# Undivided float32 operands for the first two token blocks of an attention and two-layer feed-forward kernel

## Chip, cores and metric

One core of a Trainium2 chip. The time is the device time of one execution in microseconds; 1083.91 us is the median of three runs of the kernel before (1081.91 to 1086.0).

## The reference, cut to what matters

Causal attention with a forget-gate decay for 4 batches, 8 heads, 576 positions and head size 64; its output, 2304 tokens by 512, goes through two feed-forward layers with 2048 inner columns each.

```python
scores = scale * q @ k.T + cum[:, None] - cum[None, :]     # causal, cum = cumsum(log f)
x = (softmax(scores) @ v)                                  # 2304 x 512
h = x @ w_in;   g = h * clip(h + 3, 0, 6) / 6;   x = g @ w_out
h = x @ w2_in;  g = where(h >= 1, h, where(h <= -1, 0, (h + 1) ** 2 / 4));  out = g @ w2_out
```

All of it is float32.

## The kernel before, in words

**Precision.** Most products are made on a reduced float32 type (`fp32r` in the profile), which TensorE takes in one pass. To keep the precision, both operands are divided into a rounded half and a remainder, `hi = round(a)` on ScalarE (`rounded`, line 121) and `lo = a - hi` on VectorE (`rest`, line 129), and a product is three matmuls: hi.hi, lo.hi, hi.lo (lines 560 and 607). A few products in attention (`dc` line 282, `sc` of the first jobs line 378, `av` line 474) take plain float32.

**Layers.** Layer 1 goes over 9 blocks of 256 tokens and 16 chunks of 128 inner columns: a step is one chunk of one block. `moe_h` makes `hp` (4 products of 128x128 by 256 columns), then u on ScalarE (line 567) and VectorE (line 568), then the halves of `g`. `moe_o` adds 4 products of g and the second weight to the block's sums two steps later (`LAG = 2`). After chunk 16 the sums go through `osb` (lines 627 and 625) to `x2d` in DRAM. Layer 2 takes blocks of 512 tokens in the same manner.

**Order.** `steps` holds (block, place, chunk). Blocks 0 and 1 are interleaved: block 1 follows block 0 by nine chunks (`STAG`), so that the first 32 steps, numbers 0 to 31, take both; blocks 2 to 8 follow one after another, the chunks forwards and backwards in turn. Attention is cut into pieces (scores, transposes, output) that are put between the half steps by a list of costs and due times (`cost`, `due`, `goal`); the pieces for block 0 come first of all. A scheduler places each engine's instructions from that order.

**Weights.** They come as 64-bit numbers: `w_load("raw")` fetches half a chunk (512 KB, line 157, at most four buffers `wraw`) and `w_split` converts it in a tile `wr` (ScalarE line 178, VectorE lines 179, 183, 186 and 189). For layer 1 the halves are then made into one of 12 slots `w` of 2 x 8 x 128 columns; `plan_weights` decides which chunk a slot holds at which step. Chunks that must be loaded again are kept as halves in DRAM (`wf`, `w_keep`, line 200, 1 MB) and come back by line 160. For layer 2 the converted `wr` goes to DRAM undivided through POOL's queue (line 194), in chunks from step 38 to step 105, and is loaded and divided in layer 2 ("whole"). `wr` has two buffers, which `osb` shares.

**Queues.** SP issues the loads and most stores in order. POOL makes the masks of attention (`affine_select`, lines 302, 306 and 315), which wait for the `dec` loads, and issues line 194's stores between them.

Of the kernel before, what the change touches and what calls it, by code (L numbers as in the profile page):

```python
# [8 lines left out]
F32 = mybir.dt.float32  # L9
# [7 lines left out]
P = 128  # L17
NCH = DFF // P
KD = DM // P
# [28 lines left out]
def plan_weights(visits, avail):  # L48
# [9 lines left out]
    chunk, nuse, used = [None] * n, [10**9] * n, [a - LAG - 1 if a else -LAG - 1 for a in avail]  # L58
    for t, c in enumerate(visits):
# [15 lines left out]
def tile_kernel(  # L75
# [39 lines left out]
    wsb = [wpool.tile([P, 2, 8, P], F32R, name=f"w{s}") for s in range(SLOTS)]  # L115
# [17 lines left out]
    for i in range(NCH + STAG):  # L133
        if i < NCH:
            steps.append((0, i, i))
        if i >= STAG:
            steps.append((1, i - STAG, i - STAG))
    for j in range(2, NB2):
# [4 lines left out]
    where, loads = plan_weights([c for _, _, c in steps], [0] * SLOTS + [g7] * MORE)  # L143
# [7 lines left out]
    for c, _, _, _ in loads:  # L151
        again[c] = again.get(c, -1) + 1

    def w_load(kind, c, half, s):
        if kind == "raw":
            raw = att.tile([P, 4 * P, 2], I32, tag="wraw", name="wraw", bufs=WRAW)
            nc.sync.dma_start(out=raw, in_=w[c // NCH, c % NCH, :, 8 * P * half:8 * P * half + 8 * P])
            return raw
        if kind == "parts":
            nc.sync.dma_start(out=wsb[s].bitcast(F32), in_=wf[c])  # L160
        else:
            nc.sync.dma_start(out=wsb[s][:, 1].bitcast(F32), in_=wf[c])

    def w_split(kind, c, half, s, raw):
        if kind == "parts":
            return
        if kind == "whole":
# [25 lines left out]
        if s is None:  # L193
# [269 lines left out]
    def u_out(p):  # L463
# [16 lines left out]
        for j in range(t0 // T, (t1 - 1) // T + 1):  # L480
            if (j, g) not in xt:
                xt[j, g] = moe1.tile([P, 2, T], F32R, tag="xt", name="xt", bufs=XT)
# [68 lines left out]
    def moe_h(g):  # L551
# [3 lines left out]
        ws = wsb[where[g]]  # L555
        hp = bank("hp")
        hp = hp[:, 0:w]
        for k in range(KD):
            x = xt[j, k]
            for a, bb in ((0, 0), (1, 0), (0, 1)):  # L560
                nc.tensor.matmul(  # L561
                    hp, lhsT=ws[:, a, k], rhs=x[:, bb, 0:w], start=(k == 0 and a == 0 and bb == 0),
                    stop=(k == KD - 1 and bb == 1),
                )
        u = ffn.tile([P, T2[0] if layer else T], F32, tag="u", name="u", bufs=2)[:, 0:w]
        if layer == 0:
            nc.scalar.activation(out=u, in_=hp, func=AF.Relu, bias=3.0, scale=1.0)  # L567
            nc.vector.scalar_tensor_tensor(out=u, in0=u, scalar=6.0, in1=hp, op0=ALU.min, op1=ALU.mult)  # L568
# [18 lines left out]
    def moe_o(g):  # L587
# [3 lines left out]
        ws = wsb[where[g]]  # L591
# [5 lines left out]
        if layer == 0:  # L597
# [82 lines left out]
    wq, seen = [], set()  # L680
    for c, s, free, need in loads:
# [3 lines left out]
        elif c in seen:  # L685
            wq.append((free, free, "parts", c, None, s))
        else:
            seen.add(c)
            t = free if free > 0 else max(-1, need - 6)
            wq += [(t - 3, t, "raw", c, half, s) for half in range(2)]  # L690
# [84 lines left out]
    for g in range(len(steps) + LAG):  # L775
# [74 lines left out]
```

## Time and profile before

| | |
|---|---|
| median of 3 runs | 1083.91 us |
| profiled execution, its own time | 1085.11 us |
| its span, first to last instruction | 1083.4 us |
| mean granted TensorE clock | 0.974 |
| busy: TensorE / VectorE / ScalarE / POOL | 1034.3 / 591.8 / 541.5 / 89.8 us |

In the profile PE is TensorE, DVE is VectorE, ACT is ScalarE, POOL is GpSimd, SP is the engine whose queue issues DMAs; L561 is line 561. PEclk is the granted share of TensorE's full clock, 1.00 for 2.4 GHz and 0.50 for 1.2 GHz. A busy time of TensorE is modelled at the ends of matmuls: back-to-back matmuls are best read from the starts of successive groups. Layer 1 with attention ends and layer 2 begins at about 682 us.

### The profile page before, as it was taken

The numbers are of one execution on the slowest core, as the hardware profiler recorded it, in microseconds if no ns is written. First come the engines' busy times: TensorE is split into PE (matmuls) and PEld (weight loads), VectorE is DVE, ScalarE is ACT, GpSimd is POOL, SyncE is SP. The second block draws the span as 40 slices with busy tenths as digits, with TensorE's granted clock in tenths as the row PEclk, the third lists the DMA queues.
The fourth block names the chain that finished last, engine by engine and source line by source line (L and its number), as shares of the span: only waits on it lengthen the run. The fifth ranks groups of instructions, "written<-read, shape, count | busy, mean of one in ns | idle before, by whom it ended". The sixth has DMA issues, their size and how long they took to land.

```text
span 1083.4 us, 18101 instructions
## 1 busy us (share of the span) xinstructions
PE 1034.3 (95%) x6556; PEld 903.9 (83%) x6556; DVE 591.8 (55%) x1510; ACT 541.5 (50%) x1330; POOL 89.8 (8%) x223
## 2 busy tenths in 40 slices
PE   7987999989799989999999999999999999999998
PEld 5776989979688889888989999888888888888887
DVE  7999984766577776777653436422422322332232
ACT  6877755656456655556553235533333333333343
POOL 2200010111021111121101000000100100000000
PEclk8688999999999999999999999999999999999999
DMA  8976681783586686864826035200200200010010
GB/s 235 337 222 185 213 299 54 226 277 111 182 282 197 202 298 185 282 212 123 249 68 253 2 96 167 90 1 1 77 1 1 72 6 1 19 39 1 1 40 20
DMA packets 69785, 144.20 MB, mean 133 GB/s; under 512 B 11584, under 2 KB 38720, under 8 KB 65600
## 3 DMA queue, kind: packets, MB, share of 16 engines
q1 hardware_dynamic: 67136, 134.66, 39.6%
q0 software_dynamic: 2560, 8.39, 2.0%
q8 instruction: 51, 0.84, 0.3%
q14 instruction: 38, 0.31, 0.1%
HBM read 116.74 MB, written 26.29 MB: 132 GB/s over the span
## 4 chain that ended last, share of the span: by engine, by line
PE 69%; DMA 15%; DVE 7%; issue 4%; ACT 4%; SPq 1%; POOL 0%; DVEq 0%; ACTq 0%; POOLq 0%
PE hp L561 31%; PE o L608 12%; PE o L615 10%; PE ps L615 8%; DMA qraw<-in_q 5%; DMA dec<-ncum 3%; PE pt L432 3%; DMA kraw<-in_k 2%; PE av L474 2%; DMA wraw<-in_w 2%; PE sc L388 1%; DMA x2d<-osb 1%; DMA wf<-wr 1%; DVE prob L339 1%; DVE wr L186 1%
## 5 line engine op out<-in xcount | busy, mean ns | idle before, releaser
L608 PE MATMUL o<-g,w 128*128 128x256 f32 x1728 | 250.3, 289 | 16.8 <-ACT g L121 15.3
L561 PE MATMUL hp<-xt,w 128*128 128x256 f32 x1728 | 250.6, 292 | 7.8 <-ACT w L121 5.1
L608 PEld LDWEIGHTS o<-g,w 128*128 128x128 f32 x1728 | 225.9, 191 | 26.7 <-ACT g L121 19.2
L561 PEld LDWEIGHTS hp<-xt,w 128*128 128x128 f32 x1728 | 226.8, 194 | 14.5 <-ACT w L121 6.1
L561 PE MATMUL hp<-x,w 128*128 128x512 f32 (+1 forms) x960 | 211.4, 369 | 0.0
L561 PEld LDWEIGHTS hp<-x,w 128*128 128x128 f32 x960 | 169.1, 188 | 32.5
L572 DVE SCALAR_TENSOR_TENSOR u<-hp,u 128x512 f32<-128x512 f32 (+1 forms) x80 | 50.8, 637 | 195.9 <-ACT u L571 195.9
L129 DVE TENSOR_TENSOR g<-u,g 128x256 fp32r<-128x256 f32 (+1 forms) x224 | 112.8, 505 | 71.5 <-ACT g L121 71.1
L121 ACT ACTIVATE g<-u 128x256 fp32r<-128x256 f32 (+1 forms) x224 | 106.1, 475 | 88.4 <-DVE u L572 55.3
L570 ACT ACTIVATE u<-hp 128x512 f32<-128x512 f32 (+1 forms) x80 | 44.6, 557 | 173.3 <-PE hp L561 171.5
L615 PE MATMUL o<-w,g 128*128 128x512 f32 x480 | 125.0, 396 | 0.0
L615 PEld LDWEIGHTS o<-w,g 128*128 128x128 f32 x480 | 89.1, 188 | 19.9
L345 ACT ACTIVATE prob<-prob,mx 128x512 f32<-128x512 f32 (+4 forms) x144 | 83.5, 581 | 37.4 <-DVE mx L339 37.0
L615 PE MATMUL ps<-w,g 128*128 128x512 f32 x384 | 100.4, 396 | 0.0
L568 DVE SCALAR_TENSOR_TENSOR u<-u,hp 128x256 f32<-128x256 f32 x144 | 59.4, 416 | 53.8 <-ACT u L567 53.2
L567 ACT ACTIVATE u<-hp 128x256 f32<-128x256 f32 x144 | 53.8, 378 | 67.2 <-PE hp L561 65.4
L615 PEld LDWEIGHTS ps<-w,g 128*128 128x128 f32 x384 | 72.3, 188 | 17.4
L432 PE MATMUL pt<-ident,prob 128*128 128x128 f32 (+1 forms) x400 | 69.1, 296 | 12.6 <-DVE prob L417 12.1
L339 DVE CUSTOM_DVE_ANT_0 prob<-sc,dec 128x256 f32<-128x256 f32 (+1 forms) x112 | 58.8, 533 | 25.1 <-PE sc L388 11.9
L121 ACT ACTIVATE pt<-pt 128x512 f32<-128x512 f32 (+3 forms) x160 | 61.9, 433 | 18.7 <-PE pt L432 18.2
L432 PEld LDWEIGHTS pt<-ident,prob 128*128 128x128 f32 (+1 forms) x400 | 50.3, 150 | 18.4 <-DVE prob L417 12.8
L178 ACT ACTIVATE wr<-wraw 128x512 f32<-128x512 f32 x64 | 43.0, 671 | 44.5 <-DMA wf<-wr 19.0
(76 smaller groups left out, 975.5 us busy)
## 6 DMA issues: line engine op xcount, KB each, us to landing
wraw<-in_w SPq DMA_DIRECT2D x64, 512.0 KB, 6.4
w<-wf SPq DMA_DIRECT2D x24, 1024.0 KB, 8.5
dec<-ncum SPq DMA_DIRECT2D x45, 256.0 KB, 6.6
kraw<-in_k SPq DMA_DIRECT2D x64, 144.0 KB, 3.8
wf<-w SPq DMA_DIRECT2D x8, 1024.0 KB
wf<-wr POOLq DMA_DIRECT2D x32, 256.0 KB, 6.0
w<-wf SPq DMA_DIRECT2D x16, 512.0 KB, 4.1
vv<-in_v SPq DMA_DIRECT2D x16, 320.0 KB, 10.6
```

What stands on the lines that cost most here:

```text
L121: nc.scalar.activation(out=out, in_=in_, func=AF.Copy)
L129: e.tensor_tensor(out=out, in0=in_, in1=hi.bitcast(F32), op=ALU.subtract)
L339: nc.vector.tensor_tensor_reduce(out=py[:, a:e], in0=s, in1=dc, scale=-0.125, scalar=mx[:, 2 * z:2 * z + 1] if x else 3.0e38, op0=ALU.add, ...
L345: nc.scalar.activation(out=py, in_=py, func=AF.Exp, scale=-1.0, bias=mx[:, 2 * z + x:2 * z + x + 1], accum_out=sm[:, z:z + 1],)
L432: nc.tensor.transpose(t[:nk, o:o + P], p[:, c:c + nk], ident)
L561: nc.tensor.matmul(hp, lhsT=ws[:, a, k], rhs=x[:, bb, 0:w], start=(k == 0 and a == 0 and bb == 0), stop=(k == KD - 1 and bb == 1),)
L567: nc.scalar.activation(out=u, in_=hp, func=AF.Relu, bias=3.0, scale=1.0)
L568: nc.vector.scalar_tensor_tensor(out=u, in0=u, scalar=6.0, in1=hp, op0=ALU.min, op1=ALU.mult)
L570: nc.scalar.activation(out=u, in_=hp, func=AF.Relu, bias=0.5, scale=0.5)
L572: nc.vector.scalar_tensor_tensor(out=u, in0=hp, scalar=1.0, in1=u, op0=ALU.max, op1=ALU.min)
L608: nc.tensor.matmul(o, lhsT=ws[:, a, KD + k], rhs=gg[:, bb], start=False, stop=(n == NCH - 1 and bb == 1 and k % 2 == 1),)
L615: nc.tensor.matmul(acc[j][k], lhsT=gg[:, bb, k * P:(k + 1) * P], rhs=ws[:, a, KD:2 * KD].rearrange("p k n -> p (k n)"), start=(n == 0 and ...
```

## The change

- In blocks 0 and 1 the products take undivided float32 operands, one matmul each: the weights from `nat` (8 tiles, each of two whole chunks, in the place of the slots 0 to 7), x and g without a remainder.
- `w_split` converts a layer-1 chunk straight into `nat`. After a chunk's step in block 1, `w_halves` makes its two halves (1024 columns at a time) into a slot, for the blocks from 2 on. Eleven chunks find a slot so (0 to 6, 8, 10, 12, 14); 7, 9, 11, 13 and 15 are kept undivided in DRAM (`w_keep`, 512 KB) and are loaded and divided once at need ("first"), written back as halves if they are needed again (four of them are, and so are chunks 0 to 3 after `w_halves`).
- The chunk order of blocks 2 to 8 follows from that (`back`), and `plan_weights` starts from the slots as block 1 leaves them: 41 loads in the plan instead of 56, of which 20 instead of 24 are halves of layer 1 of 1 MB.
- The raw loads and conversions of layer 1 come six steps before the chunk's step in block 0 for every chunk (chunks 12 to 15 came when a slot was free, at steps 13, 15, 17 and 19; now at 9, 11, 13 and 15).
- `wr` and `osb` share three buffers instead of two.

The diff, cut:

```diff
+    nat = [wpool.tile([P, 2, 8, P], F32, tag=f"w{s}", name=f"wn{s}") for s in range(NCH // 2)]
+    wsb = [None] * SLOTS
...
+    for c in range(NCH):
+        if spare:
+            split[c] = spare.pop(0)
+        else:
+            dropped.append(c)
+        if c % 2:
+            spare.append(c // 2)
...
+    back = [*split, *dropped]
     for j in range(2, NB2):
-        order = range(NCH) if j % 2 else range(NCH - 1, -1, -1)
+        order = back[::-1] if j % 2 else back
...
+        elif kind == "first":
+            nc.sync.dma_start(out=wsb[s][:, 1].bitcast(F32), in_=wf[c][:, 1])
...
+            if kind == "first" and again[c] > 1:
+                nc.sync.dma_start(out=wf[c], in_=wsb[s].bitcast(F32))
...
-        r = moe.tile([P, 4, P], F32, tag="wr", name="wr", bufs=2)
+        if c < NCH:
+            r = nat[c // 2][:, c % 2, ks]
+        else:
+            r = moe.tile([P, 4, P], F32, tag="wr", name="wr", bufs=3)
...
-        else:
-            rounded("a", wsb[s][:, 0, ks], r)
-            rest("v", wsb[s][:, 1, ks], r, wsb[s][:, 0, ks])
-
-    def w_keep(c, s):
-        nc.sync.dma_start(out=wf[c], in_=wsb[s].bitcast(F32))
+
+    def w_keep(c):
+        nc.sync.dma_start(out=wf[c][:, 1], in_=nat[c // 2][:, c % 2])
+
+    def w_halves(c):
+        s = split[c]
+        wsb[s] = wpool.tile([P, 2, 8, P], F32R, tag=f"w{s}", name=f"w{s}")
+        r = nat[c // 2][:, c % 2]
+        rounded("a", wsb[s][:, 0], r)
+        rest("v", wsb[s][:, 1], r, wsb[s][:, 0])
+        if c in again:
+            nc.sync.dma_start(out=wf[c], in_=wsb[s].bitcast(F32))
...
+            if j < 2:
+                rounded("a", x[:, 0, a - j * T:e - j * T], t[:, a - t0:e - t0])
+                continue
...
+            if j < 2:
+                nc.tensor.matmul(hp, lhsT=ws[:, k], rhs=x[:, 0], start=k == 0, stop=k == KD - 1)
+                continue
...
+            if j < 2:
+                gg = ffn.tile([P, 2, T], F32, tag="g", name="g", bufs=3)
+                nc.vector.scalar_tensor_tensor(out=gg[:, 0], in0=u, scalar=6.0, in1=hp, op0=ALU.min, op1=ALU.mult)
+                gt[g] = gg
+                return
...
+                if j < 2:
+                    nc.tensor.matmul(
+                        o, lhsT=ws[:, KD + k], rhs=gg[:, 0], start=False, stop=n == NCH - 1 and k % 2 == 1,
+                    )
+                    continue
...
-                o = moe.tile([P, 512], F32, tag="wr", name="osb", bufs=2)
+                o = moe.tile([P, 512], F32, tag="wr", name="osb", bufs=3)
...
+    for g, (j, _, c) in enumerate(steps[:g2]):
+        if j == 0:
+            t = max(-1, g - 6)
+            wq += [(t - 3, t, "raw", c, half, None) for half in range(2)]
...
-                    if j == 0 and again[c]:
-                        w_keep(c, where[g - LAG])
+                    if j == 0 and c in dropped:
+                        w_keep(c)
+                    if j == 1 and c in split:
+                        w_halves(c)
```

## Rows read from the trace of the kernel before

**Rows 1.** The page: busy us, share of the span, instructions; VectorE's tenths in 40 slices.
```profile
PE 1034.3 (95%) x6556; PEld 903.9 (83%) x6556; DVE 591.8 (55%) x1510; ACT 541.5 (50%) x1330; POOL 89.8 (8%) x223
...
DVE  7999984766577776777653436422422322332232
```
**Rows 2.** Windows: stretch, length, busy us of PE, PEld, DVE, ACT, POOL, clock, DMA share, GB/s.
```profile
0.00:45.00 45.00, 36.74 (x154) 25.25 (x154) 37.17 (x126) 33.29 (x99) 8.76 (x25) 0.73 0.89 277
45.00:150.00 105.00, 90.01 (x650) 81.19 (x649) 100.16 (x264) 76.37 (x201) 9.62 (x20) 0.93 0.73 225
150.00:193.00 43.00, 42.66 (x336) 39.74 (x335) 23.68 (x68) 22.34 (x62) 4.03 (x13) 1.00 0.42 144
193.00:330.00 137.00, 125.86 (x949) 112.61 (x949) 91.53 (x267) 77.20 (x215) 19.75 (x53) 0.98 0.70 218
330.00:585.00 255.00, 245.16 (x1886) 223.37 (x1885) 173.06 (x515) 148.01 (x426) 35.08 (x94) 0.98 0.64 204
```
**Rows 3.** Groups by shape (busy us, mean ns): 45 to 150 us; 0 to 45; whole span.
```profile
L129 DVE TENSOR_TENSOR w<-wr,w 128x512 fp32r<-128x512 f32 x24 | 16.4, 684 | 0.3 <-ACT w L121 0.3
L129 DVE TENSOR_TENSOR g<-u,g 128x256 fp32r<-128x256 f32 x21 | 8.8, 427 | 0.2
...
L129 DVE TENSOR_TENSOR xt<-av,xt 128x256 fp32r<-128x256 f32 x7 | 2.9, 412 | 0.7 <-ACT xt L121 0.7
...
L129 DVE TENSOR_TENSOR w<-wr,w 128x512 fp32r<-128x512 f32 x7 | 4.8, 684 | 0.2 <-ACT w L121 0.2
...
L129 DVE TENSOR_TENSOR w<-w 128x1024 fp32r<-128x1024 f32 x16 | 19.6, 1226 | 20.6 <-ACT w L121 20.6
...
L121 ACT ACTIVATE w<-w 128x1024 fp32r<-128x1024 f32 x16 | 17.0, 1061 | 20.9 <-DMA w<-wf 20.9
```
**Rows 4.** Timeline of TensorE in the steady stretch: start us, us, group.
```profile
608.43 1.60 PE L561 MATMUL hp<-xt,w 128*128 128x256 f32 x12
609.87 1.60 PE L608 MATMUL o<-g,w 128*128 128x256 f32 x12
```
**Rows 5.** Timeline of TensorE at the `dc` matmuls; the window around them.
```profile
11.50 1.57 PE L282 MATMUL dc<-upper,lf 128*128 128x256 f32 x8 [1.62 <-DVE mx L339]
13.01 0.49 PE L378 MATMUL sc<-kn,qn 64*128 64x128 f32 x4
...
12.26 0.38 PE L282 MATMUL dc<-upper,lf 128*128 128x256 f32 x1
...
12.69 0.27 PE L282 MATMUL dc<-upper,lf 128*128 128x128 f32 x1
...
12.20:12.80 0.60, 0.60 (x5) 0.55 (x5) 0.60 (x4) 0.60 (x4) 0.00 (x0) 1.00 0.60 140
```
**Rows 6.** Waits of TensorE, 45 to 193 us: us in total, times, longest.
```profile
PE o L608 <- ACT g L121: 8.7, 6, 2.3
PE hp L561 <- ACT w L121: 5.1, 3, 3.5
```
**Rows 7.** What line 178 waited for; TensorE's stops; a window after one.
```profile
  DMA wf<-wr: 19.0, 7
  DMA x2d<-osb: 12.1, 6
...
224.15 1.74 PE L608 MATMUL o<-g,w 128*128 128x256 f32 x10 [2.78 <-ACT g L121]
...
296.82 0.44 PE L432 MATMUL pt<-ident,prob 128*128 128x128 f32 x2 [3.57 <-DVE prob L417]
...
457.54 0.54 PE L432 MATMUL pt<-ident,prob 128*128 128x128 f32 x2 [2.70 <-DVE prob L417]
...
225.60:229.00 3.40, 3.40 (x15) 3.16 (x15) 2.73 (x10) 2.14 (x6) 1.36 (x3) 0.50 0.64 156
```
**Rows 8.** DMA issues of the first 45 us: KB each.
```profile
wf<-w SPq DMA_DIRECT2D x3, 1024.0 KB
```

More of the change, by code (lines that the diff above doesn't have):

```diff
@@ L45, with plan_weights @@
 AHEAD = 8100
-def plan_weights(visits, avail):
+def plan_weights(visits, avail, start):
     nxt, last = [None] * len(visits), {}
@@ L58, in plan_weights @@
     chunk, nuse, used = [None] * n, [10**9] * n, [a - LAG - 1 if a else -LAG - 1 for a in avail]
+    for s, (c, t) in start.items():
+        chunk[s], used[s] = c, t
+        if c is not None:
+            held[c], nuse[s] = s, last.get(c, 10**9)
     for t, c in enumerate(visits):
@@ L114, in tile_kernel @@
     ncum = dram.tile([B * H, S], F32, name="ncum")
-    wsb = [wpool.tile([P, 2, 8, P], F32R, name=f"w{s}") for s in range(SLOTS)]
+    nat = [wpool.tile([P, 2, 8, P], F32, tag=f"w{s}", name=f"wn{s}") for s in range(NCH // 2)]
+    wsb = [None] * SLOTS
     ident = const.tile([P, P], F32, name="ident")
@@ L137, in tile_kernel @@
             steps.append((1, i - STAG, i - STAG))
+    g2 = len(steps)
+    seen1 = {c: g for g, (j, _, c) in enumerate(steps) if j == 1}
+    split, dropped, spare = {}, [], list(range(NCH // 2, SLOTS))
+    for c in range(NCH):
[5 more added lines that the diff above has]
+            spare.append(c // 2)
+    start = {s: (c, seen1[c] - g2) for c, s in split.items()}
+    start.update({s: (None, seen1[NCH - 1] - g2) for s in spare})
+    back = [*split, *dropped]
     for j in range(2, NB2):
-        order = range(NCH) if j % 2 else range(NCH - 1, -1, -1)
+        order = back[::-1] if j % 2 else back
         for n, c in enumerate(order):
@@ L142, in tile_kernel @@
     g7 = (NB - 2) * NCH
-    where, loads = plan_weights([c for _, _, c in steps], [0] * SLOTS + [g7] * MORE)
+    where, loads = plan_weights([c for _, _, c in steps[g2:]], [0] * SLOTS + [g7 - g2] * MORE, start)
+    where = [None] * g2 + where
+    loads = [(c, s, free + g2, need + g2) for c, s, free, need in loads]
     again = {}
     for c, _, _, _ in loads:
-        again[c] = again.get(c, -1) + 1
+        again[c] = again.get(c, 0) + 1
     def w_load(kind, c, half, s):
@@ L158, in w_load @@
             return raw
+        if s is not None and kind != "raw" and wsb[s] is None:
+            wsb[s] = wpool.tile([P, 2, 8, P], F32R, tag=f"w{s}", name=f"w{s}")
         if kind == "parts":
             nc.sync.dma_start(out=wsb[s].bitcast(F32), in_=wf[c])
+        elif kind == "first":
+            nc.sync.dma_start(out=wsb[s][:, 1].bitcast(F32), in_=wf[c][:, 1])
         else:
@@ L166, in w_split @@
             return
-        if kind == "whole":
+        if kind != "raw":
             lo = wsb[s][:, 1]
@@ L192, in w_split @@
         )
-        if s is None:
+        if c >= NCH:
             nc.gpsimd.dma_start(out=wf[c][:, ks], in_=r)
-        else:
-            rounded("a", wsb[s][:, 0, ks], r)
-            rest("v", wsb[s][:, 1, ks], r, wsb[s][:, 0, ks])
-    def w_keep(c, s):
-        nc.sync.dma_start(out=wf[c], in_=wsb[s].bitcast(F32))
+    def w_keep(c):
+        nc.sync.dma_start(out=wf[c][:, 1], in_=nat[c // 2][:, c % 2])
+    def w_halves(c):
+        s = split[c]
+        wsb[s] = wpool.tile([P, 2, 8, P], F32R, tag=f"w{s}", name=f"w{s}")
+        r = nat[c // 2][:, c % 2]
[3 more added lines that the diff above has]
+            nc.sync.dma_start(out=wf[c], in_=wsb[s].bitcast(F32))
     jobs, pairs = [], []
@@ L481, in u_out @@
             if (j, g) not in xt:
[L482 removed]
+                xt[j, g] = moe1.tile([P, 2, T], F32R if j > 1 else F32, tag="xt", name="xt", bufs=XT)
             x = xt[j, g]
             a, e = max(t0, j * T), min(t1, j * T + T)
+            if j < 2:
+                rounded("a", x[:, 0, a - j * T:e - j * T], t[:, a - t0:e - t0])
+                continue
             rounded("a", x[:, 0, a - j * T:e - j * T], t[:, a - t0:e - t0])
@@ L554, in moe_h @@
         w = T2[j - NB] if layer else T
-        ws = wsb[where[g]]
+        ws = nat[c // 2][:, c % 2] if j < 2 else wsb[where[g]]
         hp = bank("hp")
@@ L590, in moe_o @@
         t0 = sum(T2[:j - NB]) if layer else j * T
-        ws = wsb[where[g]]
+        ws = nat[c // 2][:, c % 2] if j < 2 else wsb[where[g]]
         gg = gt.pop(g)
@@ L684, in tile_kernel @@
             wq.append((free, min(free + 4, need - 2), "whole", c, None, s))
-        elif c in seen:
+        elif c in dropped and c not in seen:
+            seen.add(c)
+            wq.append((free, min(free + 4, need - 2), "first", c, None, s))
+        else:
             wq.append((free, free, "parts", c, None, s))
[L687 to L690, printed above, removed]
     first = list(dict.fromkeys(c for c, _, _, _ in loads if c >= NCH))
```

## The prediction

> **What bounds the kernel now.** I read the page first, then the windows by stage, then the instructions of each stage. The page [rows 1] says TensorE 95% busy and VectorE 55%, which looks like a TensorE kernel; but the VectorE slices (27 us each) show two regimes: 9 tenths or more in slices 2 to 5, 4 in slice 7. The windows [rows 2] make that exact. From 45 to 150 us VectorE is busy 100.2 of 105 us, while TensorE has gaps and a mean granted clock of 0.93. From 150 to 193 us it turns round: TensorE 42.7 of 43, VectorE 23.7. From 193 to 585 us TensorE is busy 92 to 96% and the rest are stalls. Before 45 us VectorE (37.2 of 45), ScalarE and the DMA engines (0.89) are all close to full. The 32 steps that the change touches (blocks 0 and 1) run from about 45 to 193 us: 21 remainders of g, one for each step, lie in the first window [rows 3], the other 11 in the second.
>
> So the change trades VectorE work, which is the limit up to 150 us, for TensorE work, which is the limit from 150 us on. Its third buffer acts after 193 us.
>
> **TensorE, the price.** A divided product is three matmuls of 256 columns. In the steady stretch twelve of them start at 608.43 and the next twelve at 609.87 [rows 4]: 1.44 us, 0.120 us each, 0.36 us for three. The undivided product is a plain float32 matmul, which the trace records as two per call. Its nearest row is the `dc` matmul, the same 128x128 by 256 columns: a call starts at 12.26 and the next at 12.69, at a granted clock of 1.00 (2.4 GHz) [rows 5]. That is 0.43 us a call, 0.07 more than three divided ones. With 8 calls in a step (4 for hp, 4 for o) a step costs 8 x 0.43 - 24 x 0.12 = 0.59 us more, 32 steps 18.9 us more. Bounds: from below the same 0.43, since the two starts stand in one unbroken stream; from above the whole group with its start, 1.51 us from 11.50 to 13.01 for 768 columns [rows 5], 0.50 us per 256, which would make the 32 steps 18 us dearer still. Four calls follow each other in a step, so I take the stream.
>
> One page disagrees with the row. The Trainium skill, Perfetto Trace Analysis, section Engine Utilization, gives float32 low/high half the output rate of the array; by that an undivided call would take two passes, an estimate of 0.21 us, and TensorE would save 38 us instead of paying 18.9. Its half-rate footnote is not borne out here: the rows at 12.26 and 12.69 show twice that time at the full clock, and the sum goes by them.
>
> **VectorE and ScalarE, what leaves.** In 45 to 150 us: 24 remainders of the weights (16.4 us), 21 of g (8.8 us) and about 4 of the 7 of x (4 x 0.41 = 1.6 us) [rows 3]: 26.8 us. What comes back are the eleven late splits of the undivided weights (`w_halves`, 128x1024 each), after the step of block 1 that used the chunk: six of them by 150 us. The nearest rows are the splits of the second layer: 1226 ns on VectorE, 1061 ns on ScalarE [rows 3], so 7.4 us. VectorE goes from 100.2 to 80.8 us. ScalarE loses rounding of the same kind and at 76.4 of 105 [rows 2] isn't the bound.
>
> **45 to 150 us.** TensorE's own need: 105 us, less 13.8 us of waits for g and the weights' halves [rows 6], less 0.07 x 105 = 7.4 us lost to the half clock, is 83.8 us. 21 steps add 12.4: 96 us. VectorE needs 81. TensorE now decides, and with some 3% of waits left, as in the best later stretches [rows 2], it takes 98.5: **-6.5 us**. Bounds: -9 (no wait left) and +12.4 (no wait goes, all of TensorE's surplus on the path: the first rival).
>
> **150 to 193 us.** TensorE is full, so the other 11 steps pay in full: **+6.5 us**; VectorE's relief and the five late splits there weigh nothing (cover: VectorE is idle 19 of 43 us). Bounds 0 and +6.5.
>
> **0 to 45 us.** Seven weight remainders (4.8 us) and four of x (4 x 0.41 = 1.6 us) leave VectorE [rows 3], and three of the 1 MB weight write-backs that SP had pulled up into this stretch [rows 8] can't run there any more: they now follow `w_halves`, or are half as large and later. 3 MB at the 277 GB/s of the row [rows 2] is 11 us of DMA. All three resources are eased, but attention's own chain of small steps stays: **-4 us**, between 0 and -6.4 (VectorE's share).
>
> **193 to 585 us, the third buffer.** Converting second-layer weights writes `wr` through POOL's queue; with two buffers the next conversion waits, and as ScalarE works in order, everything behind it (u, g, the softmax) waits as well. The conversions waited 19.0 us for those writes and 12.1 us for the write of the sums [rows 7]. TensorE stood still because of it for 2.78 us at 224.15, 3.57 at 296.82 and 2.70 at 457.54 [rows 7], 9.1 us. The first stop was followed by 3.4 us at clock 0.50 [rows 7], which costs 1.7 us; taken for all three that is 5.1, so 14 us in all, and some 2 us of smaller waits. With three buffers a conversion waits for the transfer three back, so the waits behind another conversion go. The one behind the sums mostly stays: two sums and two halves follow each other, so the second half meets the first sum's buffer. Bounds 0 and -16; I take **-11**, because the next late thing (the `dec` loads that POOL's masks wait for) takes some of it.
>
> **Added after 193 us.** Five chunks (7, 9, 11, 13, 15) don't find a slot for their halves; they are kept undivided in DRAM, loaded and split once at steps 38 to 42 (5 x 1.06 us ScalarE, 5 x 1.23 us VectorE), each four steps after its load is queued, where VectorE has 45 of 137 us free [rows 2]. The later loads fall from 24 to 20 of 1 MB. On SP, the write-backs of chunks 0 to 3 and of four late ones now wait for VectorE's remainder, with q, k and `dec` loads queued behind: eight waits, each at most one split (2.3 us). Loads are issued two jobs ahead, so **+1 us**, bounds 0 and +8. SBUF slots cause no wait: a split slot reuses undivided chunks whose last reader is over two steps back. The moved conversions of chunks 12 to 15 (at steps 9 to 15 instead of 13 to 19) are the same work and take away a TensorE wait on late weights (the 5.1 us of [rows 6], counted above).
>
> **Sum** against the profiled execution (1085.1 us, 1.7 above its span, 1.2 above the median): -4 -6.5 +6.5 -11 +1 = -14, 1071; against the median **1070 us**. The layer-2 stretch is full of matmuls and unchanged.
>
> **Rivals.**
> (1) *TensorE was already the bound, and the change makes the kernel slower.* Its place is 45 to 150 us. For it: TensorE is 86% busy there. Against it: VectorE at 95% and a TensorE that waits 13.8 us for g and w. It decides if, of the 21 us of waits and half-clock loss, fewer than about 5 go (fewer than 10 with half the buffer's gain); a float32 call nearer 0.50 us works the same way. With the 18.9 us paid in full and half the buffer's gain: 1085 - 4 + 19 - 6 = 1094. The Trainium skill, Perfetto Trace Analysis, section Identifying the Most-Contended Engine, says to work for the engine of highest occupancy; over the whole span that is TensorE, which this change loads further, though the same page allows for regimes and distrusts matmul busy time. Chance 0.12.
> (2) *The third buffer moves the stall instead of removing it.* ScalarE no longer waits for `wr`, but the softmax then waits for POOL's masks and their `dec`, or SP's new waits hold those loads. Then 1085 - 4 - 6.5 + 6.5 + 1 = 1082. Chance 0.16.
> (3) *All reliefs convert*: -6.4 in the head, -9 and +6.5 in the middle, -16 behind: 1060. Chance 0.20.
> (4) *The undivided matmul takes half the time of the `dc` row.* Then TensorE falls below VectorE everywhere up to 193 us: -20 (VectorE's 81 us plus some 5% of waits) and -13 there, with -4 and -10: about 1038. The rows speak against it. Chance 0.02. It is what the Trainium skill's Perfetto Trace Analysis, section Engine Utilization, would give.
>
> **How the numbers follow.** Forecast 0.50, its own range 1062 to 1077. A measurement of this kernel can tell about 0.5% from no change, that is 1078.5 to 1089.3 us. Faster: 0.50 + 0.20 + 0.02 = 0.72; same: rival 2, 0.16; slower: rival 1, 0.12. The range runs from 1050, under rival 3 by the head's and the split's uncertainty, to 1090, over rival 2; outside are rival 4 and most of rival 1.
>
> **What would show it.** Right: in the changed profile a step of blocks 0 and 1 takes 3.47 us on TensorE back to back; VectorE well under 90% in the window of the first 21 steps, and those steps' window under 100 us; the waits of the `wr` conversion under 15 us, with no stop of TensorE over 2 us tied to them. Wrong: float32 calls at over 0.45 us back to back; TensorE still waiting for g with VectorE full; new waits of ScalarE or TensorE on `dec`, q or k after 193 us as large as the lost ones.

## The result and the profile after

The changed kernel takes **1098.7 us** (median of 4 runs, 1097.6 to 1101.8) against 1084.95 us for the kernel before, measured between them on the same chip (4 runs): a ratio of **1.0132, interval 1.0097 to 1.0168**. It is 1.3% slower, outside the forecast's range and on the other side of zero. The profiled execution took 1099.43 us with a span of 1097.7, 14.3 more than the span before.

The page of the changed kernel, part 1, to lay beside [rows 1]:

```profile
PE 1051.7 (96%) x6300; PEld 904.8 (82%) x6300; DVE 579.2 (53%) x1454; ACT 529.7 (48%) x1282; POOL 91.9 (8%) x223
```

The change did what it says: VectorE and ScalarE each lost some 12 us of work, TensorE gained 17 (forecast 19). The windows (columns as in [rows 2]), the first one up to where the first step now starts:

```profile
0.00:54.00 54.00, 38.64 (x150) 25.12 (x151) 45.11 (x139) 37.09 (x102) 11.00 (x25) 0.72 0.91 300
54.00:152.00 98.00, 94.24 (x485) 76.48 (x486) 73.42 (x200) 55.96 (x153) 7.76 (x20) 0.98 0.72 217
...
45.00:150.00 105.00, 99.28 (x505) 79.31 (x506) 81.93 (x227) 62.39 (x172) 8.74 (x20) 0.97 0.76 232
150.00:193.00 43.00, 43.00 (x221) 36.26 (x220) 18.88 (x46) 19.09 (x46) 2.88 (x10) 1.00 0.25 69
```

From 45 to 150 us VectorE fell from 100.2 to 81.9 us (forecast 80.8), and TensorE went from 90.0 to 99.3: the bound changed sides. But equal times no longer hold equal work. Each step has one `u` activation on ScalarE, and its start is a milestone. The first one in the timeline of ScalarE, before:

```profile
45.23 0.39 ACT L567 ACTIVATE u<-hp 128x256 f32<-128x256 f32 x1
```

and after:

```profile
54.11 0.38 ACT L610 ACTIVATE u<-hp 128x256 f32<-128x256 f32 x1
```

The other milestones are the `u` of step 21, 32, 48 and so on, read from the same timeline (us):

| stretch | before | after | difference | forecast |
|---|---|---|---|---|
| start to first `u` | 45.2 | 54.1 | **+8.9** | -4 |
| steps 0 to 21 | 108.6 | 97.7 | -10.9 | -6.5 |
| steps 21 to 32 | 39.0 | 48.5 | +9.5 | +6.5 |
| steps 32 to 48 | 78.5 | 84.2 | **+5.7** | +1, and part of -11 |
| steps 48 to 112 | 312.9 | 314.3 | **+1.4** | rest of -11 |
| step 112 to the end | 499.2 | 498.8 | -0.4 | 0 |

So the trade between VectorE and TensorE in the 32 steps came out near the forecast in its sum (-1.4, forecast 0), with two terms that were off by 4.4 and 3.0 us in opposite directions. Three other terms failed: the head, the new loads behind step 32, and the third buffer.

**The head.** The groups of ScalarE up to 54 us, after:

```profile
L209 ACT ACTIVATE wn<-wraw 128x512 f32<-128x512 f32 x12 | 8.1, 673 | 12.6 <-DMA wraw<-in_w 12.6
...
L126 ACT ACTIVATE w<-wn 128x1024 fp32r<-128x1024 f32 x4 | 4.2, 1042 | 0.0
```

and the same view before, up to 45 us:

```profile
L178 ACT ACTIVATE wr<-wraw 128x512 f32<-128x512 f32 x8 | 5.3, 668 | 5.1 <-DMA wraw<-in_w 5.1
```

Twelve conversions instead of eight stand ahead of the first `u`, and ScalarE waits 12.6 us for their loads instead of 5.1. Four `w_halves`, which belong behind the first steps of block 1, run there as well, with their remainders on VectorE and their 1 MB write-backs:

```profile
wraw<-in_w SPq DMA_DIRECT2D x15, 512.0 KB, 6.9
wf<-w SPq DMA_DIRECT2D x4, 1024.0 KB
```

That is the view of DMA issues up to 54 us. The write-backs are not gone, as the prediction had it; there were three [rows 8], now there are four. VectorE carries much of it: its work ahead of the first step was to shrink, and it is 45.1 us in the first 54 (the first window above) where it was 37.2 in 45 [rows 2]. The chain of waits in the head runs through both:

```profile
18.11 6.63 DMA wraw<-in_w
24.76 0.67 ACT wn L209
...
32.73 7.03 DMA wraw<-in_w
39.79 0.67 ACT wn L209
40.45 0.80 ACT prob L452 x2
...
44.16 0.88 DVE wn L217
45.04 0.34 DVE wn L210
```

Three times the chain runs through a raw load into the conversion that waits for it (the first time at 11.75 us, not shown), and behind the first and the third of these conversions into attention's softmax (`prob`), which stands behind them on ScalarE. From 43 to 52 us it runs through VectorE alone, most of it the softmax and the four instructions that finish each conversion there (lines 210, 214, 217 and 220). Which of the two sets the head's length is taken up behind its experiments.

**Behind step 32.** The timeline of ScalarE, after:

```profile
210.67 1.06 ACT L126 ACTIVATE w<-w 128x1024 fp32r<-128x1024 f32 x1 [1.96 <-DMA w<-wf]
220.16 1.06 ACT L126 ACTIVATE w<-w 128x1024 fp32r<-128x1024 f32 x1 [5.91 <-DMA w<-wf]
```

and of TensorE:

```profile
222.44 0.73 PE L661 MATMUL o<-g,w 128*128 128x256 f32 x4 [2.90 <-ACT g L126]
```

These are two of the five "first" splits. At the second, ScalarE stands 5.91 us for a load that is under way: SP issued it at 210.35 us, 3.9 us before ScalarE came to the split. The rounding of `g` is queued behind it, and TensorE stops for 2.90 us, about as long as at the stop of before that the third buffer should have removed (2.78 us, [rows 7]).

**ScalarE's waits** over the whole span, after (us in total, times, longest):

```profile
ACT wn L209 <- DMA wraw<-in_w: 36.5, 21, 4.0
...
ACT w L126 <- DMA w<-wf: 28.0, 18, 5.9
...
ACT wr L209 <- DMA x2d<-osb: 10.0, 3, 6.9
...
ACT wr L209 <- DMA wf<-wr: 8.1, 5, 4.3
```

and before:

```profile
ACT w L121 <- DMA w<-wf: 20.9, 16, 2.3
...
ACT wr L178 <- DMA wraw<-in_w: 5.6, 3, 4.6
```

The waits of the second layer's conversions for a buffer (the last two lines after) fell from 31.1 us [rows 7] to 18.1. ScalarE's waits for raw weights rose from 5.6 to 36.5, and those for stored weights from 20.9 to 28.0.

### The profile page after: what moved, and what is told of

Its sections match the earlier page's. It is cut to its first block, busy times and chain, and to the rows that moved or that the text cites. A ratio compares the mean times of both kernels' runs of the same rounds, so it can differ in the third digit from the quotient of the medians.

```text
span 1097.7 us, 17457 instructions
## 1 busy us (share of the span) xinstructions
PE 1051.7 (96%) x6300; PEld 904.8 (82%) x6300; DVE 579.2 (53%) x1454; ACT 529.7 (48%) x1282; POOL 91.9 (8%) x223
## 4 chain that ended last, share of the span: by engine, by line
PE 71%; DMA 16%; DVE 6%; issue 3%; ACT 3%; SPq 0%; POOL 0%; DVEq 0%; ACTq 0%; POOLq 0%
PE hp L604 28%; PE o L668 10%; PE o L661 10%; PE ps L668 8%; DMA wraw<-in_w 6%; DMA dec<-ncum 5%; PE hp L601 3%; PE o L656 3%; DMA qraw<-in_q 2%; PE av L511 2%; PE pt L469 2%; PE sc L425 2%; PE sc L400 1%; DMA wf<-wr 1%; DVE prob L376 1%
## 5 line engine op out<-in xcount | busy, mean ns | idle before, releaser
L661 PE MATMUL o<-g,w 128*128 128x256 f32 x1344 | 193.4, 289 | 11.3 <-ACT g L126 7.1
L604 PE MATMUL hp<-xt,w 128*128 128x256 f32 x1344 | 192.4, 291 | 3.1 <-DVE mx L376 3.1
L661 PEld LDWEIGHTS o<-g,w 128*128 128x128 f32 x1344 | 175.4, 192 | 18.3 <-ACT g L126 9.6
L604 PEld LDWEIGHTS hp<-xt,w 128*128 128x128 f32 x1344 | 175.3, 194 | 7.8 <-DVE mx L376 3.5
L126 ACT ACTIVATE g<-u 128x256 fp32r<-128x256 f32 (+1 forms) x192 | 93.2, 487 | 87.2 <-DVE u L620 55.3
L134 DVE TENSOR_TENSOR g<-u,g 128x256 fp32r<-128x256 f32 (+1 forms) x192 | 98.2, 513 | 67.4 <-ACT g L126 67.1
L382 ACT ACTIVATE prob<-prob,mx 128x256 f32<-128x256 f32 (+4 forms) x144 | 83.4, 580 | 36.5 <-DVE mx L376 35.7
L616 DVE SCALAR_TENSOR_TENSOR u<-u,hp 128x256 f32<-128x256 f32 x112 | 46.6, 418 | 46.6 <-ACT u L610 45.8
L126 ACT ACTIVATE pt<-pt 128x512 f32<-128x512 f32 (+3 forms) x160 | 61.8, 432 | 17.0 <-PE pt L469 16.4
L656 PE MATMUL o<-g,wn 128*128 128x256 f32 x256 | 65.5, 391 | 2.1 <-DVE g L613 2.1
L469 PEld LDWEIGHTS pt<-ident,prob 128*128 128x128 f32 (+1 forms) x400 | 49.6, 147 | 17.5 <-DVE prob L454 7.9
```

The costliest lines, as they stand in the source:

```text
L126: nc.scalar.activation(out=out, in_=in_, func=AF.Copy)
L134: e.tensor_tensor(out=out, in0=in_, in1=hi.bitcast(F32), op=ALU.subtract)
L382: nc.scalar.activation(out=py, in_=py, func=AF.Exp, scale=-1.0, bias=mx[:, 2 * z + x:2 * z + x + 1], accum_out=sm[:, z:z + 1],)
L469: nc.tensor.transpose(t[:nk, o:o + P], p[:, c:c + nk], ident)
L604: nc.tensor.matmul(hp, lhsT=ws[:, a, k], rhs=x[:, bb, 0:w], start=(k == 0 and a == 0 and bb == 0), stop=(k == KD - 1 and bb == 1),)
L656: nc.tensor.matmul(o, lhsT=ws[:, KD + k], rhs=gg[:, 0], start=False, stop=n == NCH - 1 and k % 2 == 1,)
```

## The experiments

"The ratio" is that to the kernel before, run in turn on the same chip; for the changed kernel it is 1.0132.

### TensorE's price

**price_alone**: the kernel before, with five more matmuls in each step of blocks 0 and 1 on the product of the two remainders (5 x 0.12 = 0.60 us a step). VectorE keeps all its work, so this is the price without the relief.

```diff
-            for a, bb in ((0, 0), (1, 0), (0, 1)):
+            for a, bb in ((0, 0), (1, 0), (0, 1)) + (((1, 1),) if j < 2 and k < 3 else ()):
...
-                for a, bb in ((0, 0), (1, 0), (0, 1)):
+                for a, bb in ((0, 0), (1, 0), (0, 1)) + (((1, 1),) if j < 2 and k % 2 == 0 else ()):
```

> The kernel before with five more matmuls (remainder times remainder, 0.12 us each) in each of the 32 steps of blocks 0 and 1: 0.60 us of TensorE a step, 19.2 us in all, and no other change. Forecast's theory (TensorE has room up to 150 us behind VectorE, none from there): 6 to 8 us slower than before, about 1092. Rival 1 (TensorE was the bound all through): 19 us slower, about 1104.

Ratio 1.0115 (1.0074 to 1.0155), +11.9 us for 19 us of matmuls: more than the 6 to 8 of the forecast's theory, less than rival 1's 19. By the milestones it is +3.7 at step 21 and +9.1 at step 32. So 21 steps hid most of their 12.6 us behind a full VectorE, and the 11 steps after them paid 5.4 of their 6.6. The two regimes of the forecast are there, though the first isn't free; rival 1, full price everywhere, doesn't hold.

**one_less**: the changed kernel without the fourth of the four hp matmuls of each step in blocks 0 and 1, whose share of the product is left out (32 x 0.43 = 13.8 us of TensorE).

```diff
-                nc.tensor.matmul(hp, lhsT=ws[:, k], rhs=x[:, 0], start=k == 0, stop=k == KD - 1)
+                if k < KD - 1:
+                    nc.tensor.matmul(hp, lhsT=ws[:, k], rhs=x[:, 0], start=k == 0, stop=k == KD - 2)
```

> The changed kernel with the fourth of the four hp products left out in blocks 0 and 1 (a quarter of the inner sum is missing there): 0.43 us of TensorE less in each of the 32 steps, 13.9 us. If TensorE is the limit through all of steps 0 to 31 of the changed kernel, as its 96% busy there says: 12 to 14 us faster, about 1086. If VectorE, ScalarE or the raw loads still set the pace up to step 21: only the last eleven steps win, 4 to 6 us, about 1093.

Ratio 1.0076 (1.0058 to 1.0093), 7.3 us off the changed kernel. Step 32 starts 9.6 us earlier, and 2 of these are lost again afterwards. That lies between the two expectations. Steps 21 to 32 win 4.1 of the 4.7 us that TensorE has less to do there, steps 0 to 21 only 4.6 of 9.0. So TensorE is the limit of the last 11 steps; in the first 21 something else stands close behind it, and no run here shows what.

### The head

Four kernels take the changed one and move its conversions or halves. "Queued behind" means that the instruction is kept, in the scheduler's order, behind the softmax exponential or the `u` that stands before it in the program.

**halves_held**: the eleven `w_halves` queued behind the `u` of their step.

```diff
...
-                        w_halves(c)
+                        with tc.issue_after(uact[0]):
+                            w_halves(c)
```

> The changed kernel, with each late split of a chunk (w_halves) queued on ScalarE behind the u of the step that calls for it, so that none can be issued in the head. Theory H (the four splits of chunks 0 to 3, 4.2 us of ScalarE, 4.9 us of VectorE and their 4 MB of write-backs, cost the head its time): the first u of block 0 comes at 48 to 50 us instead of 54.1, and the time falls by 4 to 5 us, to about 1094. Rival D (the head is held by the twelve conversions and the waits for their raw loads, the splits run beside them): first u still at 53 to 55, time within 1.5 us of the changed kernel's.

Ratio 1.0150 (1.0108 to 1.0193): nothing won. The halves left the head, and the first `u` still came at 56.1 us. The groups of ScalarE up to there show what took their place:

```profile
L209 ACT ACTIVATE wn<-wraw 128x512 f32<-128x512 f32 x15 | 10.1, 671 | 15.4 <-DMA wraw<-in_w 15.3
```

Fifteen conversions instead of twelve. My theory, that the halves and their write-backs made the head longer, fell in this form: taken away alone, they are replaced.

**lead_only**: conversions due four steps ahead instead of six, and the number set into the head eight instead of ten.

```diff
-FIRST = 10
+FIRST = 8
...
-            t = max(-1, g - 6)
+            t = max(-1, g - 4)
```

> The changed kernel with its conversions of blocks 0 and 1 due four steps before their use instead of six, and the start attached at eight instead of ten; no order against other work is written out. It is one of the two parts of head_paced (which lost 13.4 us against the changed kernel). If the number of conversions in the head decides (theory: each is work on a full VectorE and ScalarE), the first u comes at 43 us or before and the time is near 1.003 of the kernel before. If instead the conversions' place in ScalarE's order decides, a conversion in the head still stands ahead of attention's exp and waits there for its load: first u at 48 to 54, time near 1.010.

Ratio 1.0123 (1.0093 to 1.0154), first `u` at 54.0. Up to 54 us:

```profile
L209 ACT ACTIVATE wn<-wraw 128x512 f32<-128x512 f32 x12 | 8.0, 668 | 12.1 <-DMA wraw<-in_w 12.1
```

The program asked for fewer and later conversions, and the scheduler still put twelve there.

**queue_only**: due times as in the change, but the conversions queued behind.

```diff
...
+            if x[3] < NCH and x[2] == "raw":
+                with tc.issue_after(uact[0] or exps[0]):
+                    w_split(*x[2:], raw)
...
-                w_split(*x[2:], raw)
+                with tc.issue_after(exps[0]):
+                    w_split(*x[2:], raw)
```

> The other part of head_paced: conversions due six steps before their use as in the changed kernel, but each issued behind the exp or the u that stands before it in program order, so that the scheduler can't pull it ahead. If the place in ScalarE's order decides, ScalarE's waits for raw weights in the head fall from 12.6 to under 5 us and first u comes at 45 or before, time near 1.003 of the kernel before. If the number in the head decides, first u stays at 50 to 54 and the time near 1.010.

First `u` at 49.6, ratio 1.0117 (1.0053 to 1.0180). Up to 54 us:

```profile
L209 ACT ACTIVATE wn<-wraw 128x512 f32<-128x512 f32 x11 | 7.2, 665 | 3.0 <-DMA wraw<-in_w 3.0
```

The wait fell from 12.6 to 3.0 us as expected, but the first `u` gained only 4.5: the four halves are still in the head here. Neither expectation held in full, and the time can't be told from that of the changed kernel. VectorE's work up to the first `u` (the third busy time) is 40.8 us, 4.4 less than in the changed kernel:

```profile
0.00:49.58 49.58, 35.92 (x153) 24.05 (x154) 40.78 (x132) 36.02 (x102) 8.72 (x25) 0.79 0.88 279
```

**head_paced**: the three edits together.

```diff
-FIRST = 10
+FIRST = 8
...
-            t = max(-1, g - 6)
+            t = max(-1, g - 4)
...
+            if x[3] < NCH and x[2] == "raw":
+                with tc.issue_after(uact[0] or exps[0]):
+                    w_split(*x[2:], raw)
...
+                with tc.issue_after(exps[0]):
+                    w_split(*x[2:], raw)
...
+                        with tc.issue_after(uact[0]):
+                            w_halves(c)
```

> The changed kernel with the conversions of layer-1 weights and the late splits paced: eight conversions instead of twelve are due before step 0 (four steps of lead instead of six), and each is queued on ScalarE behind the exp or the u that stands before it in program order; the late splits are held as in halves_held. Theory H2 (the head grew because conversions that no longer wait for the two wr buffers are run there, twelve by the first u instead of eight; in the steps they would run beside a full TensorE for nothing): first u at 45 to 48 us instead of 54.1, and most of it is kept, 1089 to 1093 in all. Rival S (the conversions only change places: what the head wins the steps lose, as in third_alone, where the first u came 6 us later and 5.5 of them were won back by step 16): first u early, time within 3 us of 1098.7.

Ratio **1.0017 (0.9998 to 1.0037)**, 13.4 us off the changed kernel. Up to its first `u`, at 40.77 us:

```profile
L209 ACT ACTIVATE wn<-wraw 128x512 f32<-128x512 f32 x9 | 5.9, 662 | 0.6 <-DMA wraw<-in_w 0.6
...
0.00:40.77 40.77, 32.01 (x145) 21.79 (x146) 31.36 (x113) 29.67 (x92) 10.97 (x27) 0.81 0.85 248
```

Nine conversions, 0.6 us of waits, no halves, and more won than the 6 to 9 us expected. The first `u` is 4.5 us earlier than in the kernel before: the forecast's -4, once the order is held, with 5.8 us less work of VectorE (the forecast had up to 6.4). And the conversions that left the head cost little later: steps 0 to 32 take 147.0 us, against 146.2 in the changed kernel. How the last 8.8 us of the head divide between halves and due times was not tried; of the 9.4 us of work that VectorE loses from queue_only to here, 4.9 are the remainders of the four halves.

**What the head's length follows.** The same rows for nine kernels, three of which come further down (us up to the first `u`; VectorE's busy time is the third of a window's row):

| kernel | first `u` | VectorE busy | VectorE idle | ScalarE's waits for raw loads |
|---|---|---|---|---|
| before | 45.2 | 37.2 | 8.1 | 5.1 |
| before_paced | 45.1 | 36.1 | 9.0 | 0.0 |
| third_alone | 51.2 | 42.8 | 8.4 | 10.9 |
| changed | 54.1 | 45.2 | 8.9 | 12.6 |
| halves_held | 56.1 | 45.0 | 11.1 | 15.3 |
| lead_only | 54.0 | 43.2 | 10.8 | 12.1 |
| queue_only | 49.6 | 40.8 | 8.8 | 3.0 |
| head_paced | 40.8 | 31.4 | 9.4 | 0.6 |
| held3 | 38.7 | 30.8 | 7.8 | 0.5 |

VectorE is idle for 8 to 11 us in all of them, while ScalarE's waits go from 0 to 15; when queue_only took 9.6 us of these waits away, VectorE's idle time stayed. So the first `u` comes when VectorE is through with what was placed ahead of it; of the differences between the kernels, ScalarE's waits for loads can account for some 3 us at the most. No run varied VectorE's work alone, so this is read from the rows and not shown by a run of its own; a head that is long for another reason would also let more work in.

### The third buffer

**third_alone**: the kernel before with three buffers for `wr` and `osb`.

```diff
-        r = moe.tile([P, 4, P], F32, tag="wr", name="wr", bufs=2)
+        r = moe.tile([P, 4, P], F32, tag="wr", name="wr", bufs=3)
...
-                o = moe.tile([P, 512], F32, tag="wr", name="osb", bufs=2)
+                o = moe.tile([P, 512], F32, tag="wr", name="osb", bufs=3)
```

> The kernel before with three instead of two buffers for wr and the sums, nothing else. Forecast's theory: 11 us faster than before, about 1073. Rival M (the stops move to the next in-order wait): within 3 us of before. If it is faster here but not in the changed kernel, the changed kernel's own new waits eat it.

Ratio 1.0017 (0.9997 to 1.0036): nothing. Three things in its trace bear on this. First the head, ScalarE up to its first `u` at 51.2 us:

```profile
L178 ACT ACTIVATE wr<-wraw 128x512 f32<-128x512 f32 x11 | 7.4, 671 | 11.1 <-DMA wraw<-in_w 10.9
```

Eleven conversions instead of eight, 10.9 us of waits instead of 5.1, the first `u` 6 us later. The two buffers had been what kept conversions out of the head; here, with VectorE full up to step 21, what was done early was saved later (step 21 starts at 151.1, before at 153.8, and step 48 at 271.0 and 271.3). Second, its waits and one line of ScalarE's timeline:

```profile
ACT wr L178 <- DMA x2d<-osb: 10.3, 5, 6.9
ACT wr L178 <- DMA wf<-wr: 8.4, 5, 4.3
```

```profile
282.87 1.37 ACT L178 ACTIVATE wr<-wraw 128x512 f32<-128x512 f32 x2 [6.94 <-DMA x2d<-osb]
```

The waits for buffers fell from 31.1 to 18.7 us, and the time didn't: the additional buffer lets a conversion be placed earlier, and it still meets the write of the sums, for 6.94 us. Third, TensorE's stops did not go. Behind step 32 the kernel before has five of over 2 us, 13.6 us in all: the three of [rows 7], 2.31 us at 406.00 and 2.27 at 483.87. This one has four, 13.4 us in all. The first, 3.51 us at 285.64, follows the wait just shown; the others are

```profile
403.27 0.69 PE L432 MATMUL pt<-ident,prob 128*128 128x128 f32 x2 [4.10 <-DVE prob L417]
...
456.79 1.54 PE L608 MATMUL o<-g,w 128*128 128x256 f32 x6 [3.18 <-DVE g L129]
...
484.40 0.69 PE L432 MATMUL pt<-ident,prob 128*128 128x128 f32 x2 [2.56 <-DVE prob L417]
```

The chain of waits ahead of each of these three goes back to a `dec` load that was under way for 13 to 16 us. The first of them has grown out of the stop at 406.00 before, which follows a `dec` load too. VectorE's waits for `dec` over the whole span, before, here and in the changed kernel:

```profile
DVE prob L339 <- DMA dec<-ncum: 10.4, 5, 3.1
...
DVE prob L339 <- DMA dec<-ncum: 25.9, 11, 5.8
...
DVE prob L376 <- DMA dec<-ncum: 16.0, 7, 4.3
```

They come to between 5.5 and 14.5 us in the four kernels here with two buffers and to between 14.9 and 25.9 in the ten with three. So the softmax waits for `dec` where it had waited for ScalarE's conversions: the mechanism of rival 2.

**two_buffers**: the changed kernel with two buffers.

```diff
-            r = moe.tile([P, 4, P], F32, tag="wr", name="wr", bufs=3)
+            r = moe.tile([P, 4, P], F32, tag="wr", name="wr", bufs=2)
...
-                o = moe.tile([P, 512], F32, tag="wr", name="osb", bufs=3)
+                o = moe.tile([P, 512], F32, tag="wr", name="osb", bufs=2)
```

> The changed kernel with two instead of three buffers for wr and the sums. Forecast's theory (the third buffer takes ScalarE's waits away and with them stops of TensorE): 11 us slower, about 1110, with conversion waits on wf and x2d back at some 30 us. Rival M (the stops move to the next in-order wait): within 3 us of 1098.7, though the conversion waits return.

Ratio 1.0111 (1.0072 to 1.0150), 3.7 us under the changed kernel by the medians, with intervals that overlap: in the changed kernel's order the third buffer is worth nothing that shows. The conversions wait 23.3 us for buffers here, not the 30 expected, so that of the 13.0 us by which these waits fell from the kernel before to the changed one only 5.2 are the buffer's.

### The new loads behind step 32

**firsts_held**: the five "first" splits due two steps before use instead of four after the load is queued, and queued behind the `u` there.

```diff
-            wq.append((free, min(free + 4, need - 2), "first", c, None, s))
+            wq.append((free, need - 2, "first", c, None, s))
...
+            if x[2] == "first":
+                with tc.issue_after(uact[0]):
+                    w_split(*x[2:], raw)
```

> The changed kernel with the five splits of chunks loaded undivided (kind first) due two steps before need instead of four after the slot is free, and queued on ScalarE behind that step's u. Theory F (ScalarE's waits of 7.9 us for these loads, at 210 and 220 us, and the 11 us of splitting work cost block 2 its 5.7 us): steps 32 to 48 take 79 to 81 us instead of 84.2, the time falls by 3 to 5 us. Rival C (block 2 is slowed by the DMA traffic, whoever waits for it): steps 32 to 48 still 83 us or more.

Ratio 1.0066 (1.0047 to 1.0086), 8.4 us off the changed kernel. Steps 32 to 48 take 78.9 us instead of 84.2, which takes back 5.3 of the 5.7 us that had been added there, and steps 48 to 112 are 4.1 us shorter. The waits of ScalarE:

```profile
ACT w L126 <- DMA w<-wf: 20.5, 15, 2.1
```

The longest falls from 5.9 to 2.1 us, the sum to that of before.

### All of it, and what the operands are worth

**all_held** is head_paced with firsts_held and two buffers; **held3** is the same with three. The edit that both make to head_paced:

```diff
-            wq.append((free, min(free + 4, need - 2), "first", c, None, s))
+            wq.append((free, need - 2, "first", c, None, s))
...
-            if x[3] < NCH and x[2] == "raw":
+            if x[3] < NCH and x[2] != "parts":
```

> head_paced and firsts_held together, with two buffers for wr and the sums. If the parts add up (H2 6 to 9 us, F 3 to 5, two buffers 0 to 3): 1082 to 1090, no better than the kernel before. Under rivals S and C: 1093 to 1097.

> head_paced and firsts_held together, with the three buffers of the change (all_held with three instead of two). If the third buffer is worth nothing, as in third_alone and two_buffers: 1087 to 1090, like all_held. If it pays once the splits of block 2 no longer hold ScalarE (steps 32 to 48 took 87.6 us in all_held and 78.8 in firsts_held): 1074 to 1080, faster than the kernel before.

all_held: ratio 1.0054 (1.0029 to 1.0078). held3: **0.9942 (0.9923 to 0.9961)**, median 1079.0 us of 6 runs, under both kernels. They differ in the third buffer alone, and by 9.9 us in the medians, 12 by the ratios. Waits of ScalarE in all_held:

```profile
ACT wr L209 <- DMA wf<-wr: 21.6, 6, 9.3
...
ACT wr L209 <- DMA x2d<-osb: 12.1, 4, 7.5
```

and in held3:

```profile
ACT wr L209 <- DMA wf<-wr: 12.6, 4, 8.4
...
ACT wr L209 <- DMA x2d<-osb: 3.8, 4, 2.3
```

33.7 us of buffer waits become 16.4, or 23.1 with one wait of the same conversion, 6.7 us, that the profile puts down to a load of `in_q`. Most of the difference lies in steps 32 to 48, which take 87.7 us in all_held and 78.9 in held3. In all_held one conversion waits there for its buffer, and TensorE for what stands behind it; the windows of these steps are all_held's and then held3's:

```profile
217.26 0.66 ACT L209 ACTIVATE wr<-wraw 128x512 f32<-128x512 f32 x1 [9.32 <-DMA wf<-wr]
...
220.19 1.16 PE L663 MATMUL o<-g,w 128*128 128x256 f32 x3 [5.42 <-ACT g L126]
...
190.45:278.15 87.70, 79.40 (x577) 70.83 (x576) 59.04 (x160) 51.09 (x134) 12.47 (x33) 0.94 0.70 217
...
187.03:265.88 78.85, 75.47 (x578) 68.51 (x577) 59.75 (x160) 50.56 (x133) 12.50 (x33) 1.00 0.75 241
```

TensorE is idle 8.3 us instead of 3.4, and at a mean granted clock of 0.94 instead of 1.00 it is busy 79.4 us with what takes 75.5. That fits all_held, with two buffers, coming out worse than head_paced with three, against the sum of its parts. But the kernel before takes 78.5 us for these steps. The buffer repairs in held3 what all_held had lost there; it is not the gain of 11 us that the forecast saw. From step 32 to step 112 held3 is 2.0 us faster than the kernel before, and 6.6 of the 8.2 us between their spans are won before the first `u`.

**before_paced**: the kernel before with three buffers and the same pacing of its conversions.

```diff
-FIRST = 10
+FIRST = 8
...
-                o = moe.tile([P, 512], F32, tag="wr", name="osb", bufs=2)
+                o = moe.tile([P, 512], F32, tag="wr", name="osb", bufs=3)
...
-            t = free if free > 0 else max(-1, need - 6)
+            t = free if free > 0 else max(-1, need - 4)
...
+            if x[3] < NCH and x[2] == "raw":
+                with tc.issue_after(uact[0] or exps[0]):
+                    w_split(*x[2:], raw)
...
+                with tc.issue_after(exps[0]):
+                    w_split(*x[2:], raw)
```

> The kernel before with three buffers for wr and the sums and the pacing of head_paced (conversions of layer 1 due four steps before use and queued on ScalarE behind the exp or u before them). If the pacing is good whatever the operands, because the head gets shorter: first u at 40 to 43 us and 1078 to 1082. If VectorE, full from 45 to 150 us here, gives back what the head wins: 1083 to 1087. The difference to held3 is what the undivided operands are worth under the same order.

Ratio 1.0007 (0.9992 to 1.0021). Pacing and the buffer give the kernel before nothing that can be told. Its first `u` comes at 45.1 us, not at the 40 to 43 expected, although ScalarE no longer waits for raw loads ahead of it: VectorE still has 36.1 us of work there, the remainders of the weights included.

```profile
0.00:45.10 45.10, 31.75 (x155) 21.70 (x155) 36.11 (x125) 33.08 (x99) 9.38 (x25) 0.84 0.86 260
```

Between 1.0007 and 0.9942 lie 0.65%, 7 us: what the undivided operands are worth once the order is held, together with the halves, the loads and the chunk order that come with them, which were not varied alone. The first `u` comes 6.4 us earlier.

## Why the prediction was wrong, step by step

- **TensorE's price: right.** The timeline of TensorE after, in the steady stretch:

```profile
182.01 1.89 PE L601 MATMUL hp<-xt,wn 128*128 128x256 f32 x8
183.74 1.89 PE L656 MATMUL o<-g,wn 128*128 128x256 f32 x8
185.46 1.89 PE L601 MATMUL hp<-xt,wn 128*128 128x256 f32 x8
```

  From hp to hp 3.45 us for eight calls, 0.43 us each, forecast 3.47 a step. By these calls, as by the `dc` row, rival 4 is out. The half-rate footnote in the Trainium skill's Perfetto Trace Analysis, section Engine Utilization, gives half of that for a call taken as one matmul, by estimate. The trace records two matmuls a call, 0.22 us each: the footnote fits one of these records and not the call.
- **45 to 150 us, -6.5, and 150 to 193 us, +6.5: right in mechanism, both outside their bounds in size.** Steps 0 to 21 took 97.7 us (forecast 98.5 for a stretch of 105), 10.9 less than before where the bound was -9: TensorE 94.2 of 98.0 busy, clock 0.98 instead of 0.93. Steps 21 to 32 gave back 9.5, where the bound was +6.5; why more than the price of 11 steps isn't shown. That the sum is near zero as forecast is partly luck. price_alone shows the two regimes apart.
- **0 to 45 us, -4: this step failed, by 13 us.** "All three resources are eased" took for granted that the conversions would stay where they were. What had held them there was a buffer: in the kernel before a conversion needs one of two `wr`; after the change it writes into one of eight free `nat` tiles, and nothing holds it. Eight became twelve, and four halves followed. VectorE, which was to lose up to 6.4 us of work there, got 8.0 more, and the first `u` came 8.9 us later; ScalarE's waits for the loads, 12.6 us with the softmax behind them, are the smaller part of it by the table of nine kernels. third_alone shows the throttle (another buffer alone, +6 us at the first `u`), queue_only what the waits are worth (9.6 us of them gone, -4.5 at the first `u`, with VectorE's work 4.4 less), head_paced the whole (-13.3 at the first `u`, -13.4 at the end). It counts because the steps that follow are full of TensorE now: VectorE work done early saves nothing there any more. In third_alone, with VectorE as the bound, the same hoisting was neutral. With the order held, the term itself comes out: -4.5 in head_paced, and -0.1 in before_paced, where the remainders stay.
- **The third buffer, -11: failed as a term by itself.** I added up waits that the buffer would remove and took their end for time. It removed 12.4 us of them in third_alone and 5.2 in the changed kernel, and TensorE's stops came back behind the next thing in line, 13.4 us of them in third_alone for 13.6 before. Rival 2 had this mechanism, with a chance of 0.16, and named the `dec` loads as what comes next: they stand ahead of three of the four stops in third_alone. The write of the sums and, in the changed kernel, the loads of undivided chunks are others. The bounds, 0 and -16, held 0 in two pairs of kernels. The 9.9 us between all_held and held3 lie near -11 for another reason, a wait that all_held had added.
- **Added after 193 us, +1: this step failed too, +5.7.** The ends were 0 and +8. I costed the five splits as work of VectorE and ScalarE and as waits of SP; the price was ScalarE standing 5.91 us before a load that was queued four steps ahead in the program, but which SP issued 3.9 us before the split. firsts_held takes back 5.3.
- **Rival 1** gave 1094, near the measured 1098.7, for a reason that isn't the one: its place, 45 to 150 us, became faster. The rule of the Trainium skill beside it (Perfetto Trace Analysis, section Identifying the Most-Contended Engine) points at TensorE by its share of the span; here the same load on TensorE stands in held3, which is faster than the kernel before.

Open is which later wait swallows a part of what one_less saves, and what stands behind TensorE in its first 21 steps. That the order, and no other effect of the same edits, gives the head's time is shown by the counts, VectorE's work and the waits in the head; these were not varied one instruction at a time.

## What to carry to other kernels

When a change gives work a freer place to write, ask what the old buffer was holding back: a wait that goes is also an order that goes, and a scheduler that issues when buffers are free will move the work to where it is dear. Ask which engine is full in the stretch that the work moves into, and add the work to that engine; here it was VectorE. Beside the work that a load feeds, cost the engine that may stand in order before it. A sum of removed waits is an upper bound, which only the order of what comes next makes true.

## What was not expected of the hardware

A load's time from its issue to its landing varied more than I had allowed for. The page of the changed kernel gives 4.0 us as the median of the 21 loads of 512 KB of undivided weights. But 16 of them run in the second layer, where the median is 3.7 us and 40 GB/s are moved; for the five behind step 32 it is 5.9, with 212 GB/s. The one that ScalarE stood before took 9.79 us, by the chain of waits:

```profile
210.35 9.79 DMA w<-wf
```

The raw loads of the head took much the same time in two orders: 15 of them landed in a median of 6.9 us while 300 GB/s were moved, and in head_paced, up to its first `u`, ten in 6.4 us at 248 GB/s.
